# A list scheduler's priorities and durations, and the queue of some DMAs

## Chip, core and metric

The kernel runs on one core of a Trainium2 chip. The metric is the device time in microseconds (us); lower is better. The engines are TensorE (PE), VectorE (DVE), ScalarE (ACT), GpSimd (POOL) and SyncE (SP); ACT and SP also issue DMAs, each on a queue of its own. Each engine runs its own instructions in the order in which the program wrote them, and semaphores join the engines.

## What is computed

The reference takes q, k, v of 2 batches x 8 heads x 768 positions x 64 features, computes hash-bucketed attention, and passes the result through two MLPs.

```python
q_bits = (np.einsum('bhsd,dk->bhsk', q, proj) > 0)   # 6 bits, the same for k
mask = q_bucket[:, :, :, None] == k_bucket[:, :, None, :]
scores = np.where(mask, scale * np.matmul(q, kT), -1e9)
attn = exp(scores - max(scores)); attn = attn / (sum(attn) + 1e-9)
x = np.matmul(attn, v)                               # to 1536 tokens x 512
xn = x / sqrt(mean(x * x) + 1e-6) * rms_g
x = (silu(xn @ w_gate) * (xn @ w_val)) @ w_out       # d_ff 1536
h = maximum(x @ w_in, 0)
out = (h * h) @ w_out2                               # d_ff 2048
```

## The kernel before

**The work.** Attention is cut into 96 slots: 16 heads (`B*H`) by 6 tiles of 128 queries (`QT`). For each head, `plan_prep` plans the loads of k and q (`load_k`, `load_q`), their split into a high and a low part (`split_k1`, `split_q1`, `split_k2`, `split_q2`), a copy of q by DMA (`copy_q`), the product with the hash vectors (`hash_pe`), the threshold that writes the hash bits beside q (`hash_bits`), a DMA that carries k's bits beside k (`hash_dma`), and the load and scaling of v. For each slot, `plan_slot` plans the scores S (`st_S`), their maximum on DVE (`st_min`), the bias (`st_bias`), the exp (`st_exp`), the turning of the probabilities, and the product with v (`st_PV`). A slot of kind "a" splits its probabilities on ACT and POOL (`st_hi`, `st_lo`) and turns them by a DMA transpose on SP's queue (`st_T`); one of kind "x" turns them on TensorE (`st_TP`) and splits them on ACT and DVE (`st_TH`, `st_TL`).

After the eight heads of a batch, `plan_norm` computes the RMS norm (squares, a power on POOL, four small DVE steps, three diagonal scalings in `scales`, and products on TensorE that turn x). Then `products` runs through the two MLPs, with weights that `plan_weights` loads as 64-bit numbers and turns into two 32-bit parts on ACT and DVE. The first batch's MLP overlaps the second batch's attention.

**The order.** `plan_all` adds each operation to a `Plan`: a function, a rank (its priority; the unit is one slot), what it reads and writes, and the time that it is planned to take on each engine that may run it (T, D, A, P, S for TensorE, DVE, ACT, POOL, SP). `Plan.run` is a list scheduler: again and again it takes, among the operations that are ready, the one that could start first on some engine, and of equals the one of lower rank:

```python
best = (t, o.rank), n, eng, c
```

A cost given as a pair, such as `D=(0.47, H_K)`, adds its second number to the time from which that engine may be chosen. `port=True` marks operations that keep DVE and POOL from running at once in the plan. The order found is then written out: each engine gets its instructions in the planned order, and on the chip they start when their semaphores allow, whatever the planned times were. So a planned duration acts through order and choice of engine alone.

Before the change the rank of each operation comes from some 25 constants (`R_LOAD`, `R_S` and so on), the same for all heads or slots. Loads of k and q and the hash-bit DMA of heads 2 and on are issued by ACT (`LQ`, `KQ`; the hash bits from head 1), and are planned at 0.1 us of ACT each:

```python
return {"dma": cost, name: 0.475 if name == "S" else 0.1}
```

Of the kernel before, what the change touches and what calls it, by code (L numbers as in the profile page):

```python
# [23 lines left out]
RQ, RK = 64, 96  # L24
# [35 lines left out]
G = 2  # L60
# [31 lines left out]

W0 = 16
# [11 lines left out]
LQ = 'A'  # L105
KQ = 'A'
WQ = 'S'
VQ = 'S'
QQ = 'S'
# [10 lines left out]
class Plan:  # L120
# [10 lines left out]
    def __init__(self, caps):  # L131
        self.ops, self.tokens, self.bufs, self.chains, self.caps = [], {}, {}, {}, dict(caps)

    def op(self, fn, rank, r=(), w=(), new=(), use=(), dma=0.0, caps=None, chain=None, port=None,
           **costs):
# [4 lines left out]
        )  # L140
        if chain:
            o.after.add(self.chains.get(chain))
            self.chains[chain] = o
# [43 lines left out]

    def run(self):
        free = dict.fromkeys("TDAPS", 0.0)
# [6 lines left out]
        while ready:  # L196
# [22 lines left out]
            c = c[0] if isinstance(c, tuple) else c  # L219
            if o.dma:  # L220
                line = max(t + 1.25, line) + o.dma
                o.end = line
                free[eng] = line - 0.95 if c == "T" else t + c
            else:
                o.end = t + c
                if eng:
                    free[eng] = o.end
                if o.port and eng in port:
                    port[eng] = o.end
# [13 lines left out]
def tile_hash_attention_moe(  # L243
# [81 lines left out]
    def dma(name, cost):  # L325

        return {"dma": cost, name: 0.475 if name == "S" else 0.1}
# [46 lines left out]
    def plan_idle(b, r, rank, cost):  # L374

        def pe(eng):
            nc.tensor.matmul(mo(), idle[:, 0:128], idle, start=True, stop=True)

        add(pe, rank, r=r, new=[("mo", b)], T=cost)
# [5 lines left out]
    def load_k(eng, h):  # L385
        engine[eng].dma_start(out=tile_of(h, "rk", RAW, F32), in_=k[h // H, h % H])
# [269 lines left out]
    def plan_prep(h):  # L656

        s0 = QT * h
        queue = LQ if h > 1 else "S"
        add(lambda e: load_k(e, h), s0 + R_LOAD, new=[("rk", ("rk", h))], **dma(queue, 1.092))  # L660
        add(
            lambda e: load_q(e, h), s0 + R_LOAD + 0.1, new=[("rq", ("rq", h))],
            w=["begun"] * (h == 1), **dma(queue, 0.546),
# [12 lines left out]
            **(dict(D=(0.47, H_K), A=0.733, P=0.8) if h == 0 else dma(QQ, 0.6)),  # L676
        )
        for n, c in enumerate((slice(0, TB), slice(TB, S)) if h == 0 else (slice(0, S),)):
# [5 lines left out]
                P=1.8*f,  # L684
# [4 lines left out]
                P=1.8*f,  # L689
# [16 lines left out]
        else:  # L706
            b = ("hash", h)
            add(
                lambda e: hash_pe(e, h), s0 + R_HASH, T=1.4, use=[("k1", h)],
# [3 lines left out]
                lambda e: hash_bits(e, h), s0 + R_HASH, D=0.87, r=["more"] * (s_ring(h * QT + h) == "Sb"), use=[b, ("q2", h)], w=[("bits", h)],  # L713
# [3 lines left out]
                use=[("k2", h), ("q2", h)], w=[("head", h)], **dma(KQ, 0.1),  # L717
            )
        if h % VG == 0:
            add(  # L720
                lambda e: load_v(e, h), s0 + R_VL, r=["begun"] * (h > 0), new=[("vr", ("vr", h))],
                **dma(VQ if h else "S", 1.092),
            )
            for n in range(VG):
                add(
                    lambda e, n=n: bound_v(e, h, n), s0 + R_VB, use=[("vr", h)],
                    w=[("vb", h, n)], D=0.469,
                )
# [24 lines left out]
    def plan_slot(i):  # L753
# [6 lines left out]
            chain="S", T=0.72, w=[("S", i)],  # L760
        )
        if i < W1:
# [3 lines left out]
            w=[("m", i)], r=["more"] * (i < XEND), D=0.945,  # L766
        )
        add(lambda e: st_bias(e, i), i + R_BIAS, r=[("m", i)], w=[("b", i)], A=0.18, D=(0.08, H_B))
# [3 lines left out]
        if c == "x":  # L772
            for hf in range(2):
# [3 lines left out]
                    use=[("P", i)], new=[("mo", b)], T=0.35,  # L777
# [3 lines left out]
                    new=[("T" + c, ("T", i))] * (1 - hf), w=[("hi", i, hf)], A=0.39,  # L781
# [6 lines left out]
        else:  # L788
# [7 lines left out]
                **dict(P=1.7),  # L796
# [9 lines left out]
            use=[("T", i), ("vl", hx)] + [("O", hx)] * (tx > 0), w=[("PV", hx)], chain="PV",  # L806
            new=[("O", ("O", hx))] * (tx == 0), T=0.54,
# [179 lines left out]
    def plan_weights(m, rank):  # L987
        add(
            lambda e: w_load(e, m), rank, r=["begun"], new=[("wraw", ("wraw", m))],
            **dma(WQ, 1.456),  # L990
# [249 lines left out]
    def plan_all():  # L1240
# [4 lines left out]
        add(lambda e: nc.sync.dma_start(out=cst, in_=small), -40, w=["cst"], **dma("S", 0.056))  # L1245
# [102 lines left out]
```

## Time and profile before

| | |
|---|---|
| median of 3 runs | 823.69 us (823.62 to 825.3) |
| the profiled execution: its time | 821.74 us |
| the profiled execution: its span | 819.5 us |
| granted TensorE clock, mean over the span | 0.985 |
| busy: PE, DVE, ACT, POOL | 778.5, 689.3, 459.3, 220.2 us |

The span goes from the first instruction to the last; the time has some 2 us more around it. Busy times are sums over the whole span, and the kernel has stages with different limits, so they are to be read stage by stage. Issuing a DMA is not counted as busy. "PEld" is the loading of weights into TensorE, which overlaps its products. A granted clock of 1.00 is 2.4 GHz; its other level is 1.2 GHz, and a number between them is a mean over a stretch.

### The profile page before, as it was taken

Reading aid. Unit: us, or ns where it says so; the run is one execution under the profiler, and the core shown is the slowest. Engines: PE = TensorE matmul, PEld = TensorE weight load, DVE = VectorE, ACT = ScalarE, POOL = GpSimd, SP = SyncE. Lnnn points to the kernel's source line nnn. Section 1 sums busy time; section 2 is a strip of 40 time slices with the busy share of each in tenths; the row PEclk is TensorE's granted clock in tenths of the full one; section 3 lists DMA queues with packets and bytes.
Section 4 is the critical chain, followed back from the end, with each engine's and each line's share of the span. In section 5 each row is a group of like instructions: output and inputs, shape, how many; then the busy total and the mean of one; then the engine's idle time right before and its main releaser. Section 6 shows DMA issues by size and latency. Waiting matters only on the chain.

```text
span 819.5 us, 14924 instructions
## 1 busy us (share of the span) xinstructions
PE 778.5 (95%) x5633; PEld 724.0 (88%) x5633; DVE 689.3 (84%) x1369; ACT 459.3 (56%) x931; POOL 220.2 (27%) x187
## 2 busy tenths in 40 slices
PE   7889887999999898999999999999999999999998
PEld 4888776899888897999989999999899899998996
DVE  6997979899888889999998989999487797777764
ACT  5888878768788777443554433466534242342320
POOL 7488956457557544000000000000000000000000
PEclk8999999899999999999999999999999999999999
DMA  7576884689969998232253333422221130211004
GB/s 215 164 133 147 164 181 125 129 173 184 248 146 193 180 198 189 78 103 103 103 180 129 104 128 105 154 104 103 76 79 52 52 104 26 78 52 52 26 1 154
DMA packets 127728, 100.69 MB, mean 123 GB/s; under 512 B 106548, under 2 KB 108596, under 8 KB 127656
## 3 DMA queue, kind: packets, MB, share of 16 engines
q1 hardware_dynamic: 124160, 90.92, 43.4%
q10 hardware_dynamic: 3496, 8.81, 3.7%
q8 instruction: 44, 0.72, 0.4%
q14 instruction: 28, 0.23, 0.1%
HBM read 67.12 MB, written 3.15 MB: 86 GB/s over the span
## 4 chain that ended last, share of the span: by engine, by line
PE 71%; DVE 18%; ACT 3%; DMA 3%; issue 3%; POOL 1%; SPq 0%; ACTq 0%; DVEq 0%; POOLq 0%
PE mo L1012 34%; PE mo L1132 16%; PE mo L1121 9%; PE S L549 5%; PE O L623 4%; DVE Pa L560 2%; DVE Px L560 2%; DMA wraw<-in_w 1%; DVE Tx L314 1%; DVE q L437 1%; PE S L428 1%; PE mo L878 1%; ACT xall L645 1%; DMA Ta<-hla 1%; DVE acc L1146 1%
## 5 line engine op out<-in xcount | busy, mean ns | idle before, releaser
L314 POOL TENSOR_TENSOR hla<-Pa,hla 128x768 f16<-128x768 f32 x66 | 110.0, 1669 | 69.9 <-ACT hla L305 62.9
L1146 DVE TENSOR_TENSOR acc<-acc,mo 128x512 f32<-128x512 f32 (+1 forms) x164 | 101.2, 617 | 27.7 <-PE mo L1132 23.1
L549 PE MATMUL S<-k,q 76*128 76x384 f32 (+1 forms) x384 | 93.2, 368 | 12.9 <-DVE Pa L560 7.3
L1045 ACT ACTIVATE mt<-mo 128x384 f32<-128x384 f32 x64 | 31.4, 490 | 103.8 <-PE mo L1012 101.6
L309 POOL TENSOR_SCALAR yh<-mu 128x384 fp32r<-128x384 f32 x19 | 11.4, 602 | 276.3 <-PE mo L1132 152.4
L549 PEld LDWEIGHTS S<-k,q 76*128 76x128 f32 (+1 forms) x384 | 66.8, 196 | 19.9 <-DVE Pa L560 9.4
L1132 PE MATMUL mo<-woh,yl 128*128 128x512 f32 x192 | 75.3, 392 | 0.0
L1132 PE MATMUL mo<-wol,yh 128*128 128x512 f32 x192 | 75.2, 392 | 0.0
L1132 PE MATMUL mo<-woh,yh 128*128 128x512 f32 x192 | 74.7, 389 | 0.0
L560 DVE TENSOR_SCALAR_CACHE_REDUCE Pa<-S 128x768 f32<-128x768 f32 x66 | 62.7, 950 | 9.2 <-PE S L549 8.6
L956 ACT ACTIVATE wv<-wraw 128x512 f32<-128x512 f32 x82 | 54.1, 669 | 22.5 <-DMA wraw<-in_w 21.7
L1049 DVE TENSOR_TENSOR mu<-mt 128x384 f32<-128x384 f32 x64 | 35.4, 553 | 36.5 <-ACT mt L1045 36.5
L314 DVE TENSOR_TENSOR yl<-mu,yh 128x384 fp32r<-128x384 f32 x112 | 60.8, 551 | 6.0 <-POOL yh L309 4.4
L1121 PE MATMUL mo<-yl,woh 128*128 128x384 f32 x192 | 64.9, 338 | 0.6 <-DVE yl L314 0.6
L1121 PE MATMUL mo<-yh,woh 128*128 128x384 f32 x192 | 65.2, 340 | 0.0
L1121 PE MATMUL mo<-yh,wol 128*128 128x384 f32 x192 | 65.0, 338 | 0.0
L578 ACT ACTIVATE Pa<-Pa,b 128x768 f32<-128x768 f32 x66 | 62.0, 943 | 4.4 <-DVE sum L638 0.9
L305 ACT CAST hla<-Pa 128x768 f16<-128x768 f32 x66 | 55.0, 835 | 4.6 <-DVE sc L509 1.2
L976 DVE SCALAR_TENSOR_TENSOR wv<-wraw,wv 128x512 uint32<-128x512 uint32 x82 | 57.2, 699 | 0.4
L305 ACT CAST wih<-wv 128x512 fp32r<-128x512 f32 x42 | 26.2, 623 | 55.8 <-DVE wv L976 55.5
L972 DVE SCALAR_TENSOR_TENSOR wv<-wraw,wv 128x512 uint32<-128x512 uint32 x82 | 56.4, 690 | 0.7
L1012 PE MATMUL mo<-xTAh,wih 128*128 128x384 f32 x160 | 54.4, 340 | 0.0
(170 smaller groups left out, 2285.7 us busy)
## 6 DMA issues: line engine op xcount, KB each, us to landing
wraw<-in_w SPq DMA_DIRECT2D x104, 512.0 KB
rk<-in_k ACTq DMA_DIRECT2D x14, 384.0 KB
vr<-in_v SPq DMA_DIRECT2D x8, 384.0 KB
out<-acc SPq DMA_DIRECT2D x12, 256.0 KB
q<-q SPq DMA_DIRECT2D x15, 192.0 KB
rq<-in_q ACTq DMA_DIRECT2D x14, 192.0 KB
Ta<-hla SPq DMA_TRANSPOSE x66
rk<-in_k SPq DMA_DIRECT2D x2, 384.0 KB
```

Of the source, the lines that this page charges most:

```text
L305: nc.scalar.copy(out_, in_)
L314: engine[eng].tensor_tensor(out=out_, in0=in0, in1=in1, op=ALU.subtract)
L549: nc.tensor.matmul(sp[:, hf, 0:TB], d[a][0:kr, t * 128:(t + 1) * 128], d[b2][0:kr, hf * TB:(hf + 1) * TB], start=(n == 0), stop=(n == 1),)
L560: nc.vector.tensor_scalar(out=e["P"].rearrange("p (a b) -> p a b", a=2), in0=e["sp"][:, :, 0:TB], scalar1=-1e9 / SCALE, scalar2=None, op0= ...
L578: nc.scalar.activation(e["P"], e["P"], AF.Exp, bias=e["b"], scale=SCALE)
L956: nc.scalar.activation(t, f32(wst[m]["hi"]), AF.Abs)
L972: nc.vector.scalar_tensor_tensor(out=t, in0=hi, scalar=0xC0000000, in1=t, op0=ALU.bitwise_and, op1=ALU.bitwise_or)
L976: nc.vector.scalar_tensor_tensor(out=t, in0=lo, scalar=29, in1=t, op0=ALU.logical_shift_right, op1=ALU.bitwise_or)
L1012: nc.tensor.matmul(ps, a[:, c * 128:(c + 1) * 128], b2[:, c, :], start=(c == 0 and n == 0), stop=(c == 3 and n == 2),)
L1121: nc.tensor.matmul(po, a[:, dc * 128:(dc + 1) * 128], b2, start=(j == 0 and n == 0), stop=(j == len(fs) - 1 and n == 2),)
L1132: nc.tensor.matmul(po, a[:, tt * 128:(tt + 1) * 128], b2, start=(j == 0 and n == 0), stop=(j == len(fs) - 1 and n == 2),)
L1146: nc.vector.tensor_tensor(out=ac, in0=ac, in1=st["p"], op=ALU.add)
```

## The change

The planned durations of some operations are changed, and DMA issues on ACT get planned durations of their own. Loads of k and q and the hash-bit DMA may be issued by SP, or by ACT where its start, with `H_ACT` = 3.0 us added, is earlier. A plan keeps account of narrow and wide products on TensorE and adds `SWITCH` where a wide one follows a narrow one. All engines are planned free from 0.72 us. A table, `SHIFTS`, holds one 16-bit number for each planned operation; divided by 32 it is added to the operation's rank (`Plan.shift`). It has 3,212 numbers, of which 2,159 are not zero; the last of these is number 2,179.

```diff
--- before.py
+++ after.py
@@ -1,4 +1,6 @@
+import base64
 import math
+import zlib
 from collections import deque
 from contextlib import ExitStack
 
@@ -90,6 +92,7 @@
 R_AFT = -10.9
 
 
+SWITCH = 0.085
 W0 = 16
 W1 = 13
 
@@ -102,11 +105,64 @@
 H_K = 2.7
 H_V = 1
 H_VL = 2.0
-LQ = 'A'
-KQ = 'A'
-WQ = 'S'
-VQ = 'S'
-QQ = 'S'
+H_ACT = 3.0
+
+
+SHIFTS = (
+    'c-rk(_jgs*v!A{9Dfiwa5K%y?fK;i%L#6p80x>iNgP?#QEkH#0ieLdkF-WNT6(JCc2nt9OkYYe7Dj<mTA}s+Wgb-o~x1'
...
+)
 
 
 class Op:
@@ -130,14 +186,16 @@
 
     def __init__(self, caps):
         self.ops, self.tokens, self.bufs, self.chains, self.caps = [], {}, {}, {}, dict(caps)
+        self.wide = None
 
     def op(self, fn, rank, r=(), w=(), new=(), use=(), dma=0.0, caps=None, chain=None, port=None,
-           **costs):
+           wide=True, **costs):
 
 
         o = Op(
             fn, rank, costs, dma, new, use, caps or {}, chain, "P" in costs if port is None else port
         )
+        o.wide = wide
         if chain:
             o.after.add(self.chains.get(chain))
             self.chains[chain] = o
@@ -185,8 +243,16 @@
                     t = max(t, u.end + self.delay(u, eng))
         return t
 
+    def shift(self):
+        raw = zlib.decompress(base64.b85decode(SHIFTS)) if SHIFTS else bytes(2 * len(self.ops))
+        assert len(raw) == 2 * len(self.ops)
+        for n, o in enumerate(self.ops):
+            moved = int.from_bytes(raw[2 * n:2 * n + 2], "little", signed=True)
+            o.rank = (round(o.rank * 32) + moved) / 32 + n % 97 * 1e-6
+
     def run(self):
-        free = dict.fromkeys("TDAPS", 0.0)
+        self.shift()
+        free = dict.fromkeys("TDAPS", 0.72)
         line = 0.0
         port = {"D": 0.0, "P": 0.0}
         taken = {ring: [] for ring, _, _ in self.bufs.values()}
@@ -217,6 +283,9 @@
             o = ready.pop(n)[0]
             o.eng, o.start = eng, t
             c = c[0] if isinstance(c, tuple) else c
+            if eng == "T":
+                c += SWITCH * (o.wide and self.wide is False)
+                self.wide = o.wide
             if o.dma:
                 line = max(t + 1.25, line) + o.dma
                 o.end = line
@@ -322,9 +391,9 @@
     def junk():
         return pers.tile([128, 512], F32, tag="wv", name="wv", bufs=WV)
 
-    def dma(name, cost):
-
-        return {"dma": cost, name: 0.475 if name == "S" else 0.1}
+    def dma(cost, act=None, sync=0.475):
+
+        return {"dma": cost, "S": sync, **({"A": (act, H_ACT)} if act else {})}
 
 
     banks = deque([mops] * 3)
@@ -376,7 +445,7 @@
         def pe(eng):
             nc.tensor.matmul(mo(), idle[:, 0:128], idle, start=True, stop=True)
 
-        add(pe, rank, r=r, new=[("mo", b)], T=cost)
+        add(pe, rank, r=r, new=[("mo", b)], T=cost, wide=False)
 
     def tile_of(h, name, n=3, dtype=F32R):
         t = heads[h][name] = ap.tile([128, S], dtype, tag=name, name=name, bufs=n)
@@ -656,11 +725,14 @@
     def plan_prep(h):
 
         s0 = QT * h
-        queue = LQ if h > 1 else "S"
-        add(lambda e: load_k(e, h), s0 + R_LOAD, new=[("rk", ("rk", h))], **dma(queue, 1.092))
-        add(
-            lambda e: load_q(e, h), s0 + R_LOAD + 0.1, new=[("rq", ("rq", h))],
-            w=["begun"] * (h == 1), **dma(queue, 0.546),
+        begun = ["begun"] * (h > 1)
+        add(
+            lambda e: load_k(e, h), s0 + R_LOAD, r=begun, new=[("rk", ("rk", h))],
+            **dma(1.092, 0.42 if h > 1 else None),
+        )
+        add(
+            lambda e: load_q(e, h), s0 + R_LOAD + 0.1, r=begun, new=[("rq", ("rq", h))],
+            w=["begun"] * (h == 1), **dma(0.546, 0.55 if h > 1 else None, 0.55),
         )
         add(
             lambda e: split_k1(e, h), s0 + R_K1, use=[("rk", h)], new=[("k1", ("k1", h))],
@@ -673,7 +745,7 @@
         add(
             lambda e: copy_q(e, h), s0 + R_QC, use=[("rq" if h == 0 else "q1", h)],
             new=[("q2", ("q2", h))], w=[("qc", h)],
-            **(dict(D=(0.47, H_K), A=0.733, P=0.8) if h == 0 else dma(QQ, 0.6)),
+            **(dict(D=(0.47, H_K), A=0.733, P=0.8) if h == 0 else dma(0.6)),
         )
         for n, c in enumerate((slice(0, TB), slice(TB, S)) if h == 0 else (slice(0, S),)):
             f = 0.55 if h == 0 else 1.0
@@ -681,12 +753,12 @@
                 lambda e, c=c: split_k2(e, h, c), s0 + R_K2, use=[("rk", h), ("k1", h)],
                 r=[("k2", h)] if n else [], w=[("k2", h, n)] + [("k2", h)] * (n == 0),
                 new=[("k2", ("k2", h))] * (n == 0), D=(0.87 * f, H_SUB), port=True,
-                P=1.8*f,
+                P=1.9 * f,
             )
             add(
                 lambda e, c=c: split_q2(e, h, c), s0 + R_Q2, use=[("rq", h), ("q1", h)],
                 w=[("ql", h, n)], D=(0.87 * f, H_SUB), port=True,
-                P=1.8*f,
+                P=1.9 * f,
             )
         if h == 0:
             for hf in range(2):
@@ -706,25 +778,25 @@
         else:
             b = ("hash", h)
             add(
-                lambda e: hash_pe(e, h), s0 + R_HASH, T=1.4, use=[("k1", h)],
+                lambda e: hash_pe(e, h), s0 + R_HASH, T=1.39, use=[("k1", h)],
                 r=["wz", ("ql", h, 0), ("k2", h, 0)], new=[(s_ring(h * QT + h), b)],
             )
             add(
-                lambda e: hash_bits(e, h), s0 + R_HASH, D=0.87, r=["more"] * (s_ring(h * QT + h) == "Sb"), use=[b, ("q2", h)], w=[("bits", h)],
+                lambda e: hash_bits(e, h), s0 + R_HASH, D=1.117, r=["more"] * (s_ring(h * QT + h) == "Sb"), use=[b, ("q2", h)], w=[("bits", h)],
             )
             add(
                 lambda e: hash_dma(e, h), s0 + R_HDMA, r=[("bits", h)],
-                use=[("k2", h), ("q2", h)], w=[("head", h)], **dma(KQ, 0.1),
+                use=[("k2", h), ("q2", h)], w=[("head", h)], **dma(0.1, 0.82, 0.8),
             )
         if h % VG == 0:
             add(
                 lambda e: load_v(e, h), s0 + R_VL, r=["begun"] * (h > 0), new=[("vr", ("vr", h))],
-                **dma(VQ if h else "S", 1.092),
+                **dma(1.092),
             )
             for n in range(VG):
                 add(
                     lambda e, n=n: bound_v(e, h, n), s0 + R_VB, use=[("vr", h)],
-                    w=[("vb", h, n)], D=0.469,
+                    w=[("vb", h, n)], D=0.462,
                 )
             b = ("vb", h)
             add(
@@ -757,15 +829,15 @@
         ko = [(x, h) for x in ("k1", "q1", "k2", "q2")]
         add(
             lambda e: st_S(e, i), i + R_S, use=ko, r=[("head", h), ("qc", h)] + [("bits", 0, 1, 0)] * (h == 0 and t >= TT), new=[(s_ring(i), ("S", i))],
-            chain="S", T=0.72, w=[("S", i)],
+            chain="S", T=0.7, w=[("S", i)],
         )
         if i < W1:
             plan_idle(("idle S", i), [("S", i)], i + R_S, 0.22)
         add(
             lambda e: st_min(e, i), i + R_MIN, use=[("S", i)], new=[("P" + c, ("P", i))],
-            w=[("m", i)], r=["more"] * (i < XEND), D=0.945,
-        )
-        add(lambda e: st_bias(e, i), i + R_BIAS, r=[("m", i)], w=[("b", i)], A=0.18, D=(0.08, H_B))
+            w=[("m", i)], r=["more"] * (i < XEND), D=0.9,
+        )
+        add(lambda e: st_bias(e, i), i + R_BIAS, r=[("m", i)], w=[("b", i)], A=0.105, D=(0.08, H_B))
         add(
             lambda e: st_exp(e, i), i + R_EXP, r=[("b", i)], use=[("P", i)], w=[("exp", i)], A=0.827
         )
@@ -774,11 +846,11 @@
                 b = ("PT", i, hf)
                 add(
                     lambda e, hf=hf: st_TP(e, i, hf), i + R_TP, r=[("exp", i), "ident"],
-                    use=[("P", i)], new=[("mo", b)], T=0.35,
+                    use=[("P", i)], new=[("mo", b)], T=0.327, wide=False,
                 )
                 add(
                     lambda e, hf=hf: st_TH(e, i, hf), i + R_TH, r=space, use=[b] + [("T", i)] * hf,
-                    new=[("T" + c, ("T", i))] * (1 - hf), w=[("hi", i, hf)], A=0.39,
+                    new=[("T" + c, ("T", i))] * (1 - hf), w=[("hi", i, hf)], A=0.357,
                 )
                 add(
                     lambda e, hf=hf: st_TL(e, i, hf), i + R_TL, r=[("hi", i, hf)],
@@ -793,7 +865,7 @@
             add(
                 lambda e: st_lo(e, i), i + R_LO, r=[("hi", i)], use=[("P", i), ("hl", i)],
                 w=[("lo", i)], D=(0.87, H_PLO), port=True,
-                **dict(P=1.7),
+                P=1.63,
             )
             add(
                 lambda e: st_T(e, i), i + R_T, r=[("lo", i)] + space,
@@ -803,8 +875,8 @@
         lows = [("lo", i, 0), ("lo", i, 1)] if c == "x" else []
         add(
             lambda e: st_PV(e, i), i + R_PV, r=[("v", hx)] + space + lows,
-            use=[("T", i), ("vl", hx)] + [("O", hx)] * (tx > 0), w=[("PV", hx)], chain="PV",
-            new=[("O", ("O", hx))] * (tx == 0), T=0.54,
+            use=[("T", i), ("vl", hx)] + [("O", hx)] * (tx > 0), w=[("PV", hx)], chain="PV", wide=False,
+            new=[("O", ("O", hx))] * (tx == 0), T=0.548,
         )
         x = i
         m = TT if hx % H == H - 1 else QT
@@ -987,7 +1059,7 @@
     def plan_weights(m, rank):
         add(
             lambda e: w_load(e, m), rank, r=["begun"], new=[("wraw", ("wraw", m))],
-            **dma(WQ, 1.456),
+            **dma(1.456),
         )
         b = ("wv", m)
         far = apart(m)
@@ -1242,7 +1314,7 @@
             nc.vector.memset(warm, 0.0)
             nc.scalar.activation(warm, warm, AF.Exp)
 
-        add(lambda e: nc.sync.dma_start(out=cst, in_=small), -40, w=["cst"], **dma("S", 0.056))
+        add(lambda e: nc.sync.dma_start(out=cst, in_=small), -40, w=["cst"], **dma(0.056))
         add(constants, -40, A=2.3, w=["warm"])
         add(lambda e: nc.vector.memset(idle, 0.0), -40, D=0.1, w=["idle"])
         for n in range(W0):
```

## Rows read from the trace of the kernel before

**Rows 1.** Busy time of each engine by stage: stretch, its length, busy and instructions.

```profile
core 0: us, PE busy (x) PEld busy (x) DVE busy (x) ACT busy (x) POOL busy (x), PEclk, DMA share, GB/s
0.00:13.50 13.50, 8.34 (x26) 3.64 (x27) 7.81 (x27) 5.46 (x8) 8.40 (x15) 0.91 0.62 162
13.50:20.00 6.50, 6.50 (x28) 5.20 (x27) 4.34 (x9) 4.84 (x10) 6.13 (x5) 0.67 1.05 326
20.00:140.00 120.00, 105.05 (x1328) 94.09 (x1326) 105.23 (x229) 103.39 (x240) 82.92 (x69) 0.99 0.70 156
140.00:150.00 10.00, 7.96 (x55) 7.28 (x54) 7.87 (x16) 6.01 (x15) 6.01 (x5) 0.66 0.53 99
150.00:180.00 30.00, 27.82 (x271) 25.97 (x270) 28.12 (x52) 24.17 (x49) 14.91 (x13) 0.94 0.68 142
180.00:340.00 160.00, 149.53 (x1406) 140.60 (x1405) 140.65 (x286) 122.85 (x252) 88.12 (x61) 0.99 0.86 181
340.00:430.00 90.00, 87.57 (x497) 85.42 (x495) 84.56 (x169) 42.56 (x77) 3.25 (x5) 1.00 0.36 123
430.00:815.80 385.80, 385.76 (x2036) 361.77 (x2036) 310.08 (x588) 150.07 (x287) 10.51 (x17) 1.00 0.24 82
815.80:819.50 3.70, 0.00 (x0) 0.00 (x0) 0.69 (x1) 0.00 (x0) 0.00 (x0) 1.00 0.37 142
```

**Rows 2.** Timeline of TensorE at 150 us: start, length, line, operation.

```profile
149.95 0.33 PE L1012 MATMUL mo<-xTAh,wih 128*128 128x384 f32 x1
```

**Rows 3.** ACT's DMA issues by line: shortest, median, longest ns; first and last start.

```profile
L386 ACTq DMA_DIRECT2D rk<-in_k x14: 329/333/359, 10.7 to 211.4; - x14
...
L389 ACTq DMA_DIRECT2D rq<-in_q x14: 473/514/1128, 0.9 to 213.2; - x14
...
L445 ACTq DMA_DIRECT2D k<-q x15: 736/788/1335, 23.8 to 272.7; - x15
```

**Rows 4.** DMA queues from 20 to 140 us: packets, MB, share; and one issue.

```profile
q1 hardware_dynamic: 32263, 12.66, 53.0%
q10 hardware_dynamic: 2332, 5.86, 16.4%
...
k<-q ACTq DMA_DIRECT2D x9, 36.0 KB
```

**Rows 5.** Timeline of ACT at 83 us, with one hash-bit issue.

```profile
83.07 0.94 ACT L578 ACTIVATE Px<-Px,b 128x768 f32<-128x768 f32 x1
84.02 0.75 ACTq L445 DMA_DIRECT2D k<-q  x1
84.88 0.94 ACT L578 ACTIVATE Pa<-Pa,b 128x768 f32<-128x768 f32 x1 [0.86 <-DVE sum L638]
```

**Rows 6.** Instructions grouped by line and form: busy us, mean ns, idle before.

```profile
L314 POOL TENSOR_TENSOR hla<-Pa,hla 128x768 f16<-128x768 f32 x66 | 110.0, 1669 | 69.9 <-ACT hla L305 62.9 <-issue 4.6 <-DMA rk<-in_k 1.8
...
L314 POOL TENSOR_TENSOR k<-rk,k 128x768 fp32r<-128x768 f32 x13 | 24.2, 1858 | 5.7 <-DVE k L307 3.7 <-ACT k L305 1.7
...
L314 POOL TENSOR_TENSOR q<-rq,q 64x768 fp32r<-64x768 f32 x13 | 23.7, 1826 | 1.2 <-ACT q L305 0.3
...
L437 DVE TENSOR_SCALAR q<-S,cst 44x768 fp32r<-44x768 f32 x15 | 16.3, 1086 | 3.3 <-PE S L428 3.0
```

**Rows 7.** Waits of SP's queue: us in total, times, longest.

```profile
SPq L943 <- DVE wv L976: 381.8, 75, 19.6
SPq L590 <- POOL hla L314: 93.6, 39, 6.8
```

**Rows 8.** Timeline of SP's queue at 120 us.

```profile
120.59 2.13 SPq L590 DMA_TRANSPOSE Ta<-hla  x1
```

**Rows 9.** Waits of TensorE from 20 to 140 us.

```profile
PE S L549 <- DVE q L437: 4.4, 7, 1.5
```

**Rows 10.** Timeline of DVE at 140 us.

```profile
140.14 3.49 DVE L869 TENSOR_SCALAR diag<-ident,rr 128x128 f32<-128x128 f32 x3
```

**Rows 11.** Chain of waits at 415 us: start, us, what.

```profile
414.74 3.73 DMA wraw<-in_w
```

52 lines of the change are left out of this document (added).

## Prediction

> **What bounds the kernel now.** I read the stage table first. [rows 1] cuts the span of 819.5 us where the work changes. TensorE idles 819.5 - 778.5 = 41.0 us, and nearly all of it lies early: 5.2 us before 13.5 us, 15.0 between 20 and 140, 4.2 between 140 and 180, 10.5 between 180 and 340, 2.4 between 340 and 430, then 0.04 in 386 us, and 3.7 in the last store. From 430 us on TensorE alone sets the time, and no order of its fixed work can shorten that stretch. A better order can win only before it.
>
> Between 20 and 140 us the attention of the first eight heads runs, and the first product of the MLP cannot start before it is normalised; the first one stands at 149.95 us [rows 2]. In this stage no engine's busy time fills the 120 us: DVE has 105.2, TensorE 105.1, ACT 103.4, POOL 82.9. But issuing a DMA holds an engine without counting as busy. ACT issues three for each head, with medians of 0.333 (k), 0.514 (q) and 0.788 us (hash bits) [rows 3]; nine of each fall into this stage [rows 4], so 9 x 1.635 = 14.7 us. [rows 5] shows one: exp ends, a hash-bit issue of 0.75 us stands alone, ACT is idle for 0.86 us, and the next exp follows. The releaser named there (DVE sum) is the last semaphore seen, not the cause. Busy and issuing together, ACT has 118.1 of 120 us: ACT sets this stage. Between 180 and 340 us no engine is so full: TensorE 149.5 of 160, DVE 140.7, ACT 122.9 [rows 1], with TensorE's idle time spread over waits of about a microsecond.
>
> **The change, part by part.** All arithmetic stays: the same instructions with the same shapes. The edits move instructions between queues and in the order of each queue.
>
> *Planned durations.* The old plan gives ACT 0.1 us for each DMA issue; the rows above say 1.635 us a head, so the old plan misses about 1.3 us of ACT in each of 14 or 15 heads. The new one takes 0.42, 0.55 and 0.82. It raises the hash threshold from 0.87 to 1.117 us (measured 1.086) and the k2/q2 subtractions on POOL from 1.8 to 1.9 (1.858 and 1.826), and lowers POOL's low half from 1.7 to 1.63 (1.669) [rows 6]. These alone cost nothing on the chip; they make the order fit better, and I give them no term of their own.
>
> *Queues.* k, q and the hash bits now take SP unless ACT could start over 3 us earlier (H_ACT). Where SP is busy with transposes some stay on ACT. If all leave, ACT falls to 103.4 us in the first stage and DVE, at 105.2, is next. DVE cannot fill a stage wholly: the densest mixed stage of [rows 1] is 150 to 180 us, with 28.12 of 30, or 94%. At 94% DVE needs 105.2 / 0.94 = 111.9 us: **8 us** gained of a ceiling of 120 - 105.2 = 14.8; the other end is nothing, if the moved issues stay or their transfers come late. I take 8.
>
> What hides the moved issues is SP's spare time, and SP is an in-order queue too. It waits 93.6 us in 39 waits for POOL's low halves before it can transpose, 2.4 us each and 6.8 at the longest [rows 7]; a transpose then holds it for some 2.1 us [rows 8]. Behind such a wait the three DMAs of a head would be late: k and q are loaded well ahead by their ranks, so they have slack; the hash bits have little, since the head's first S waits for them. Today S waits 4.4 us, in 7 waits, with the hash threshold as releaser [rows 9]. I give this no cost in the sum, because the planner treats SP as in order, and its whole price to a rival.
> In 20 to 140 us SP's queue has 53.0% of the DMA engines' time and ACT's 16.4% [rows 4]. The Trainium skill (DMA: Bandwidth & Descriptors, section on queues, rings and completion order) says that each of the two queues has its own rings, that a ring is consumed in order, and that an engine takes turns between rings. By that, a load moved to SP loses its turn and stands behind the transposes; this speaks against the move, and would take from the 8 us what a late k or q costs. The rows show no such load, so I leave the 8.
>
> *The table.* It holds 3,212 numbers, one for each planned operation; 2,159 are not zero, all among the first 2,180: attention, normalisation and the first part of the MLP. Half of these move a priority by more than 25.8 slots (there are 96 slots). A priority decides only between operations that could start at the same moment on an engine, so this is a new choice almost everywhere before about 430 us, and none after. Its gain is bounded by the idle time and lost clock of the stages.
> - 140 to 180 us: idle 4.2 us, and a granted clock of 0.66 over 10 us and 0.94 over 30, worth 3.4 + 1.8 = 5.2 us at full clock: together 9.4. Three diagonal scalings hold DVE for 3.49 us [rows 10], and the chain square, power, scaling, product stays as it is; only other heads' work can fill the gap. I take **4 us**, under half.
> - 180 to 340 us: idle 10.5 us, clock loss 160 x 0.01 = 1.6. With DVE at 94% instead of 88% its 140.7 us would fit in 149.6, also 10.4 less. Both are ceilings; I take **5 us**.
> - 340 to 430 us: 2.4 us idle, as weights land late (3.73 us in the chain [rows 11]). Their loads stay on SP, where they wait 381.8 us in 75 waits for DVE to free a buffer [rows 7], and the later ones have a zero in the table: 0, between 0 and 2.4.
> - 0 to 20 us: the first loads and their order of need are the same: 0, within 2 us either way.
>
> *Narrow and wide products.* SWITCH adds 0.085 us to the plan where TensorE goes from a narrow product to a wide one. It costs the chip nothing; the search can now see that switches cost.
>
> **The sum.** 8 + 4 + 5 = 17 us: a span of 802.5 us. Around the span lie 821.74 - 819.5 = 2.24 us, so the profiled execution would take 804.7; it stood 1.95 us below the median of 823.69, so the median would be 806.7. I forecast 806.
>
> **The rivals.**
> *Slower: the SP queue.* Hash bits behind a transpose that waits for POOL. It speaks for it that SP waits so often, and against it that the plan models the order. If each of 15 heads loses half of a mean wait, 1.2 us, with nothing to cover it, that is 18 us; the first stage's 8 go too, the 9 of the others stay: 823.7 - 9 + 18 = 833. At 17 / 15 = 1.1 us a head, against the whole 17, it decides the sign.
> *No change: the plan doesn't hold on the chip.* A table found in a model fits its errors. The three scalings are still planned at 0.2 us each, against 3.49 in all [rows 10]; such stretches, not in the plan, shift everything behind them, and the in-order queues cannot reorder. Then the old waits are replaced by new ones of the same total: 822 to 824. A part of it, with 2 to 8 us left of the gain, gives 816 to 822.
> *Much faster.* If the search packs all stages to their ceilings: 14.8 + 9.4 + 12.1 + 2.4 = 38.7 us, so 785; with most of it, about 790. For it speaks the number of operations that it moves, against it that DVE and TensorE would both have to be full.
> TensorE's 105.1 us busy between 20 and 140 stand beside 94.1 us of weight loads, and 149.5 beside 140.6 between 180 and 340 [rows 1]. The Trainium skill (Trainium Kernel Development and Optimization, section on performance expectations) calls matmul busy time a bad metric and weight-load busy time a good one. By that the third stage has 160 - 140.6 = 19.4 us to give instead of 10.5, and the ceiling falls by 9 us to 776. DVE stops the stage first by the rows, so I count 0.02 of this case's chance to it.
>
> **Chances.** Forecast, a gain of 8 to 26 us (798 to 816): 0.60. Much faster: 0.12. A small gain (816 to 822): 0.10. No change: 0.06. Slower: 0.12. A measurement of this kernel tells about 0.2%, or 1.6 us, from no change. So faster 0.82, same 0.06, slower 0.12. The range of 790 to 822 leaves out the slower case, half of no change and a little of the ceiling: 2 in 10. The likeliest case's own range is 798 to 816.
>
> **What would show it.** Right: under half of the 27 ACT issues left in the first stage; the first MLP product at about 140 us instead of 150; TensorE's idle time down from 41 to some 25 to 28 us, with the stretch after 430 as long as before for the same products; fewer stretches below full clock before 240 us. Wrong: SP's waits grow and S waits longer for the hash bits (the queue rival); ACT is relieved, but DVE's idle time grows as much (the model rival); or the first product comes earlier but the weights or DVE hold TensorE up after 340 us, so that the gain is given back later.

## The result, and the profile after

The changed kernel takes 804.81 us (median of 4 runs, 800.63 to 807.46) against 824.50 us for the kernel before beside it (4 runs, 823.62 to 826.37). The ratio is 0.9754, with a 95% interval of 0.9707 to 0.9800: a gain of 19.7 us, where 17 were forecast. The profiled execution took 800.63 us, with a span of 798.8. It is the fastest of the four, so what its stages show lies on the good side; a second profiled execution of the same kernel (the changed kernel again, below), with a span of 805.8, is named beside it.

The stages of the changed kernel, in the columns of [rows 1]:

```profile
0.00:13.50 13.50, 11.07 (x39) 5.64 (x39) 9.94 (x32) 5.43 (x7) 8.80 (x15) 1.00 0.58 162
13.50:20.00 6.50, 3.48 (x20) 2.79 (x21) 3.79 (x9) 4.05 (x8) 4.15 (x4) 1.00 0.96 305
20.00:140.00 120.00, 110.92 (x1368) 100.00 (x1369) 109.34 (x242) 112.71 (x264) 94.37 (x78) 0.96 0.77 166
140.00:150.00 10.00, 10.00 (x103) 9.52 (x102) 9.38 (x19) 7.02 (x11) 5.47 (x5) 1.00 0.81 116
150.00:180.00 30.00, 27.88 (x257) 26.64 (x254) 29.50 (x56) 21.39 (x43) 17.00 (x13) 1.00 0.91 216
180.00:340.00 160.00, 152.05 (x1422) 144.98 (x1422) 142.02 (x286) 119.84 (x243) 86.53 (x65) 1.00 0.81 169
340.00:430.00 90.00, 90.00 (x522) 90.00 (x521) 85.90 (x173) 46.39 (x86) 3.32 (x5) 1.00 0.38 130
430.00:795.10 365.10, 365.05 (x1918) 341.06 (x1917) 291.76 (x555) 137.66 (x264) 12.27 (x20) 1.00 0.24 81
795.10:798.80 3.70, 0.00 (x0) 0.00 (x0) 0.68 (x1) 0.00 (x0) 0.00 (x0) 0.96 0.37 142
sum 798.80, PE 770.46 PEld 720.62 DVE 682.31 ACT 454.50 POOL 231.90; mean PE 85.61 PEld 80.07 DVE 75.81 ACT 50.50 POOL 25.77
```

Read the last long stretch first. From 430 us on TensorE is full, as before: 365.10 / 1918 = 0.190 us for each of its instructions, and 385.80 / 2036 = 0.189 before [rows 1]. Nothing was gained there; 118 of these instructions had simply been done already. So the whole gain was made before 430 us.

How much in which stage? TensorE loses time in two ways: by standing idle, and by running below its full clock, which is the length times one less the granted clock (at most that, since idle time inside the stretch is counted in both). Fixed stretches of time cut the work of the two kernels at different places (the normalisation of the first batch moved from beyond 140 us to before it), so the first four stretches are taken together:

| TensorE's loss, us | before: idle + clock | after: idle + clock | gained |
|---|---|---|---|
| 0 to 150 | 22.2 + 7.9 | 14.5 + 4.8 | 10.8 |
| 150 to 340 | 12.7 + 3.4 | 10.1 + 0.0 | 6.0 |
| 340 to 430 | 2.4 + 0.0 | 0.0 + 0.0 | 2.4 |

That is 19.2 of the span's 20.7 us; the clock is shown to two digits only. The second execution gives 6.6, 2.2 and 2.4 us by the same count, 11.2 of the 13.7 by which its span is shorter. Each part loses less in both; how much each gives differs by several us. Over the whole span idle time went from 41.0 to 28.3 us (32.3 in the second execution), and the mean clock from 0.985 to 0.993 (0.989).

The DMA issues that ACT still has between 20 and 140 us, from its timeline:

```profile
29.22 0.33 ACTq L455 DMA_DIRECT2D rk<-in_k  x1
73.34 0.49 ACTq L458 DMA_DIRECT2D rq<-in_q  x1
110.01 0.33 ACTq L455 DMA_DIRECT2D rk<-in_k  x1
```

Three are left of 27 [rows 4]: 1.2 us in place of 14.7. ACT is nevertheless still the fullest engine of the stage. Its busy time rose from 103.4 to 112.7 us, because 264 instructions now fit instead of 240. With its issues that makes 113.9 of 120 us, or 95%; TensorE has 110.9, or 92%, and DVE 109.3, or 91%. Cut where the norm's first squares begin (below), the stage shows what the issues did: before, ACT has 98.6 us of its own work and 14.7 of issues in the 115.2 us from 20 us on; after, 100.9 and 1.2 in 105.7. ACT fills 98% of the first stretch and 97% of the second. It had some 11 us less to do, and the stretch is 9.5 shorter.

The waits of SP's queue in the changed kernel, to be held against [rows 7]:

```profile
SPq L1015 <- DVE wv L1048: 387.7, 74, 19.6
SPq L659 <- POOL hla L383: 53.7, 30, 5.2
```

And TensorE's wait for the hash bits from 20 to 140 us, against [rows 9]:

```profile
PE S L618 <- DVE q L506: 0.4, 1, 0.4
```

SP's waits for POOL's low halves fell from 93.6 to 53.7 us although it took over the issues (in the first experiment below, which keeps the old order, they are 55.0, so the fall goes with the move), and S waits for hash bits for 0.4 us instead of 4.4.

Two marks of progress, by line: the squares of the RMS norm on ACT, which begin as soon as the attention of the first half of the first batch's positions is done, and the first kind of MLP product (shortest, median, longest ns; first and last start in us):

```profile
L912 ACT ACTIVATE wv<-xall x12: 614/630/657, 125.7 to 325.1; 128x512 f32<-128x512 f32 x12
...
L1084 PE MATMUL mo<-xTAh,wih x160: 333/334/427, 144.8 to 775.9; 128*128 128x384 f32 x160
```

The squares begin at 125.7 us; before it was 135.2. The first product starts at 144.8 instead of 149.95 [rows 2]. (In the second execution they stand at 128.2 and 147.9.) Of 9.5 us won by the squares, 4.4 don't show at the first product: 19.1 us lie between the two now, 14.7 before. But the first product does not mark the same progress in both kernels. The norm is done in two halves of three tiles of positions each, and the first MLP product on the second half (xTB) has moved much further:

```profile
L1012 PE MATMUL mo<-xTBh,wih x160: 332/334/423, 170.0 to 798.7; 128*128 128x384 f32 x160
...
L1084 PE MATMUL mo<-xTBh,wih x160: 332/334/423, 147.5 to 778.0; 128*128 128x384 f32 x160
```

It starts at 147.5 instead of 170.0. The new order puts the whole second half of the norm ahead of the first product, the 24 products that turn its x too; before, these ran between 160 and 170 us:

```profile
141.37 2.25 PE L950 MATMUL mo<-diag,xall 128*128 128x128 f32 x18
...
144.17 0.83 PE L950 MATMUL mo<-diag,xall 128*128 128x128 f32 x6
```

So the longer way to the first product holds work that came later before. POOL lengthens it as well, as this stretch of DVE and POOL shows:

```profile
136.64 0.15 DVE L929 TENSOR_TENSOR rt<-rr 128x3 f32<-128x3 f32 x1
136.83 1.50 DVE L931 TENSOR_TENSOR rt<-rt,ss 128x3 f32<-128x3 f32 x1
138.36 1.58 DVE L933 TENSOR_SCALAR rt<-rt 128x3 f32<-128x3 f32 x1
139.97 0.81 DVE L937 TENSOR_TENSOR rr<-rr,rt 128x3 f32<-128x3 f32 x1
140.89 0.68 DVE L941 TENSOR_SCALAR diag<-ident,rr 128x128 f32<-128x128 f32 x3
141.49 0.61 DVE L387 SCALAR_TENSOR_TENSOR xTAl<-mo,cst,xTAh 128x384 fp32r<-128x384 f32 x1
...
136.66 3.25 POOL L383 TENSOR_TENSOR hla<-Pa,hla 128x768 f16<-128x768 f32 x2
139.86 0.90 POOL L383 TENSOR_TENSOR vl<-vr,ones 128x384 f16<-128x384 f32 x1
```

Four steps on three columns take 0.14 to 0.16 us each where nothing holds them (the kernel before, from 138.60 to 140.11 us), as the first one does here. The second ends at 138.33, half-way through POOL's pair of subtractions. The third ends at 139.94, as the pair ends at 139.91; the fourth at 140.78, as POOL's next one ends at 140.76. These steps belong to the second half of the norm, but DVE's queue is in order, and the low parts of the turned x (xTAl), which the first product needs, stand behind them.

### The profile page after: what moved, and what is told of

It reads as the page before. It is cut to its first block, busy times and chain, and to the rows that moved or that the text cites. A ratio compares the mean times of both kernels' runs of the same rounds, so it can differ in the third digit from the quotient of the medians.

```text
span 798.8 us, 14938 instructions
## 1 busy us (share of the span) xinstructions
PE 770.5 (96%) x5633; PEld 720.6 (90%) x5633; DVE 682.3 (85%) x1365; ACT 454.5 (57%) x922; POOL 231.9 (29%) x200
## 4 chain that ended last, share of the span: by engine, by line
PE 59%; DVE 0%; ACT 0%; issue 0%
PE mo L1084 33%; PE mo L1204 16%; PE mo L1193 9%; PE mo L950 1%; DVE acc L1218 0%; ACT xall L714 0%
## 5 line engine op out<-in xcount | busy, mean ns | idle before, releaser
L1218 DVE TENSOR_TENSOR acc<-acc,mo 128x512 f32<-128x512 f32 (+1 forms) x164 | 100.9, 618 | 28.4 <-PE mo L1204 23.1
L618 PE MATMUL S<-k,q 76*128 76x384 f32 (+1 forms) x384 | 87.1, 354 | 7.3 <-DVE Pa L629 6.2
L618 PEld LDWEIGHTS S<-k,q 76*128 76x128 f32 (+1 forms) x384 | 65.0, 190 | 10.8 <-DVE Pa L629 8.3
L378 POOL TENSOR_SCALAR yh<-mu 128x384 fp32r<-128x384 f32 x25 | 14.1, 569 | 199.9 <-PE mo L1204 88.4
L383 DVE TENSOR_TENSOR yl<-mu,yh 128x384 fp32r<-128x384 f32 x112 | 65.4, 590 | 6.1 <-POOL yh L378 5.2
L378 POOL TENSOR_SCALAR wih<-wv 128x512 fp32r<-128x512 f32 x11 | 7.2, 658 | 174.1 <-ACT mt L1117 109.7
L1044 DVE SCALAR_TENSOR_TENSOR wv<-wraw,wv 128x512 uint32<-128x512 uint32 x82 | 56.0, 687 | 0.4
L1048 DVE SCALAR_TENSOR_TENSOR wv<-wraw,wv 128x512 uint32<-128x512 uint32 x82 | 55.9, 684 | 0.2
```

The costliest lines, as they stand in the source:

```text
L383: engine[eng].tensor_tensor(out=out_, in0=in0, in1=in1, op=ALU.subtract)
L618: nc.tensor.matmul(sp[:, hf, 0:TB], d[a][0:kr, t * 128:(t + 1) * 128], d[b2][0:kr, hf * TB:(hf + 1) * TB], start=(n == 0), stop=(n == 1),)
L1044: nc.vector.scalar_tensor_tensor(out=t, in0=hi, scalar=0xC0000000, in1=t, op0=ALU.bitwise_and, op1=ALU.bitwise_or)
L1048: nc.vector.scalar_tensor_tensor(out=t, in0=lo, scalar=29, in1=t, op0=ALU.logical_shift_right, op1=ALU.bitwise_or)
L1218: nc.vector.tensor_tensor(out=ac, in0=ac, in1=st["p"], op=ALU.add)
```

## The experiments

All gains below are against the kernel before in the same group of runs: 824.04 us for the first three kernels, 823.00 for the next three, 822.95 for the last four.

**The issues alone, in the order of before.** Every DMA that ACT issues is issued by SP instead, at the same place of the order.

```diff
-            o.fn(o.eng)
+            o.fn("S" if o.dma and o.eng == "A" else o.eng)
```

> The order of the kernel before on every compute engine, but the 43 DMA issues of ACT (k, q, hash bits) are issued by SP at their place in the planned sequence. Theory (ACT's issue time sets the first stage): about 8 us less, 814 to 819 us, with the squares of the first batch starting some 5 to 9 us earlier than 135.2 us. Rival of the SP queue: hash bits come late behind waiting transposes, 825 us or more, S waits longer for the hash bits. Rival that the order alone counts: 822 to 825 us.

Measured: 820.54 us, ratio 0.9962 (0.9930 to 0.9993), a gain of 3.5 us. Its squares by line:

```profile
L840 ACT ACTIVATE wv<-xall x12: 612/620/637, 129.9 to 325.4; 128x512 f32<-128x512 f32 x12
```

They begin 5.3 us earlier than before, with no new plan. TensorE's waits from 20 to 140 us, of which the slower rival spoke:

```profile
PE S L549 <- DVE q L437: 3.4, 5, 1.5
...
PE S L549 <- DMA k<-q: 1.0, 1, 1.0
```

One wait of 1.0 us for a hash-bit transfer, even where nothing was planned for it. Moving the issues pays by itself, clear of no change, but not for the 8 us that were expected.

**The change without the table.**

```diff
-SHIFTS = (
...
-)
+SHIFTS = ""
```

> The changed kernel with all numbers of the table zero: new durations, new choice of queue, old ranks. Theory: keeps the 8 us of the first stage and loses the 9 of the other two, about 813 to 817 us. Rival that the table does it all: 821 us or more. Rival that queues and durations do it all: 804 to 808 us.

Measured: 815.78 us, ratio 0.9893 (0.9851 to 0.9935), a gain of 8.3 us. Durations and queues give these, with the smaller edits that stay in (`SWITCH`, the start at 0.72 us, the `begun` condition on later loads); the table gives the rest. Its squares start at 124.8 us, no later than with the table, and its first product on the second half at 159.1.

**The changed order, with the issues on ACT.** Every DMA that the change lets choose is issued by ACT.

```diff
-            o.fn(o.eng)
+            o.fn("A" if o.dma and "A" in o.costs else o.eng)
```

> The order of the changed kernel on every compute engine, but all k and q loads of heads 2 and on and all hash-bit DMAs are issued by ACT at their place in the sequence. Theory: ACT has 118 us of work again in the first stage, so 8 us or more are lost, 812 to 820 us. Rival that the table alone counts: 804 to 808 us.

Measured: 809.44 us, ratio 0.9824 (0.9768 to 0.9881): 4.6 us above the changed kernel's first series and 3.4 above its longer one (below), both of other groups, and the intervals overlap. So the loss of 8 us or more that was expected did not come. The squares stand where ACT's load puts them:

```profile
L912 ACT ACTIVATE wv<-xall x12: 616/628/656, 131.7 to 331.8; 128x512 f32<-128x512 f32 x12
```

That is 6.0 us later than in the changed kernel, or 3.5 later than in its second execution, against 5.3 us earlier in the first experiment. Both directions say that the issues delay the first batch's attention by 3.5 to 6 us.

**The durations alone.** No table, and the movable DMAs are planned and issued on ACT, with their new durations; the smaller edits named above stay in.

```diff
-        return {"dma": cost, "S": sync, **({"A": (act, H_ACT)} if act else {})}
+        return {"dma": cost, **({"A": act} if act else {"S": sync})}
```

> New durations (0.42, 0.55 and 0.82 us for ACT's issues among them) and SWITCH, table of zeros, k, q and hash-bit DMAs on ACT as before. With the table zero and the choice of queue the time was 815.8 us. Theory: ACT's issues leave the first stage only with the queue, so this gives 818 to 822 us, some 4 us more than with the choice. Rival that honest durations do most of the 8 us by themselves: 814 to 817 us. Rival that durations don't matter: 822 to 826 us.

Measured: 820.75 us, ratio 0.9964 (0.9924 to 1.0004), a gain of 2.3 us that is not clear of nothing. Its squares start at 134.8 us, 0.4 earlier than before: by themselves the durations do not shorten the first stage. The free choice of queue is worth 8.3 - 2.3 = 6.0 us within a plan that knows the durations, a difference of two groups whose intervals overlap a little.

**The table for part of the time.** The shifted ranks are used up to a planned time, and the old ones from there on, once with `CUT = 130` and once with 340.

```diff
+                    rank = o.rank if t < CUT else o.base
...
-                        best = (t, o.rank), n, eng, c
+                        best = (t, rank), n, eng, c
```

Up to 130:

> The changed kernel, but the planner uses the table's ranks only for operations that it places before 130 us of its own clock, and the old ranks after. Bounds from the runs so far: 815.8 us without the table, 804.8 with it. If the table's gain is made in the first stage: 805 to 808 us. If it is made by the overlap of attention and MLP after it, as the prediction's 4 + 5 us say: 812 to 817 us.

Up to 340:

> As the one before, with the table's ranks until 340 us of the planner's clock and the old ranks after. If the table's gain lies before the pure MLP stretch: 803 to 808 us, as with the whole table. If its last part, which orders the first part of the MLP, matters: 809 us or more.

Measured: 814.59 us (0.9806 to 0.9936) up to 130, a gain of 8.4; 805.55 us (0.9709 to 0.9812) up to 340, a gain of 17.5. Used up to 130 us the table adds next to nothing to the 8.3 us without it. Its use from 130 to 340 us adds 9.0 us to that, and the runs of the two kernels lie apart (812.9 to 816.52 and 805.03 to 806.71). Whether the table for 130 to 340 alone would give as much was not tried, nor was any single move of it, so by what moves it wins its 9 us stays open.

**The table on the plan of before.** With the old durations and queues the same table leads to no order at all: at some point every operation that is ready waits for a buffer that none of the ready ones frees. So it has no time, but it shows that these numbers cannot be carried to that plan.

**The changed kernel again**, in the group of the three that follow.

> The changed kernel itself again, as the measure for the other three of this call: 804.8 us, between 800 and 808, since its single runs so far lie that far apart.

Measured: 806.04 us (6 runs, 803.64 to 809.04), ratio 0.9786 (0.9754 to 0.9818), a gain of 16.9 us.

**Without three of POOL's subtractions.** For slots 49 to 51 POOL writes zeros in place of the low half of the probabilities; the rest is unchanged.

```diff
         hl = tiles[i]["hl"]
+        if i in (49, 50, 51):
+            nc.gpsimd.memset(hl[:, 1, :], 0.0)
+            return
         sub(eng, hl[:, 1, :], tiles[i]["P"], hl[:, 0, :])
```

> The changed kernel, with the low half of slots 49, 50 and 51 (the ones that POOL subtracts while the first norm runs) filled with zeros by POOL instead of being computed. Theory (POOL's subtraction of 128x768 holds DVE's small steps of the norm): the steps that take 1.50 and 1.58 us take some 0.15, the first norm's products come 2 to 4 us earlier after the squares, 800 to 803 us. Rival (something else stretches them): the steps stay long, 804 to 806 us.

Measured: 803.16 us (0.9729 to 0.9784), 2.9 us below the unedited kernel of the same group, with intervals that overlap. DVE's steps and POOL in the unedited kernel:

```profile
139.81 1.50 DVE L931 TENSOR_TENSOR rt<-rt,ss 128x3 f32<-128x3 f32 x1
141.34 1.58 DVE L933 TENSOR_SCALAR rt<-rt 128x3 f32<-128x3 f32 x1
...
139.64 3.25 POOL L383 TENSOR_TENSOR hla<-Pa,hla 128x768 f16<-128x768 f32 x2
```

And with the zeros:

```profile
138.62 0.16 DVE L934 TENSOR_TENSOR rt<-rt,ss 128x3 f32<-128x3 f32 x1
138.81 1.06 DVE L936 TENSOR_SCALAR rt<-rt 128x3 f32<-128x3 f32 x1
...
138.44 1.42 POOL L656 MEMSET hla<- 128x768 f16 x2
```

The stretched steps repeat to the digit in another execution, and shrink with POOL's work: that POOL holds DVE there is shown. From squares to first product it is 16.5 us instead of 19.6 in the unedited run, against 14.7 in the kernel before. So POOL's subtractions make some 3 us of that stretch; the rest of the difference is put down to the order.

**The norm planned with POOL.** The four steps and the scalings get `port=True`, which keeps them from lying beside POOL in the plan, and the table is searched anew for that plan.

```diff
-            add(lambda e, n=n: newton(e, hf, n), R_X, r=[("rr", hf)], w=[("rr", hf)], D=0.08)
+            add(lambda e, n=n: newton(e, hf, n), R_X, r=[("rr", hf)], w=[("rr", hf)], D=0.09, port=True)
...
-                D=0.2,
+                D=0.21, port=True,
```

> The planner is told that the three-column steps and the diagonal scalings of the norm can't run beside POOL's work (port), and the table is searched anew for that plan. If the unplanned stretch in the norm is what the changed kernel loses: 797 to 802 us. If a new table is worth no more than the old one on the chip: 803 to 807 us.

Measured: 807.04 us (0.9764 to 0.9839), no better than the changed kernel. On the chip a step still took up to 1.45 us and a scaling up to 1.69, so the plan did not keep them clear of what lengthens them. The table is also another one, and the two cannot be told apart here.

**The table searched further**, with nothing else changed.

> The same planner as in the changed kernel and its table searched further, nothing else. If each step that the search finds is kept on the chip: 800 to 803 us. If further search only fits the plan: 804 us or more, and above the kernel whose plan knows the norm.

Measured: 800.25 us (6 runs, 798.46 to 808.22), ratio 0.9732 (0.9693 to 0.9771): 5.8 us below the changed kernel in the same group, with intervals that overlap. It has the lowest median of all versions here.

## Why the prediction held, point by point

**Where time can be won: right.** Nothing was won after 430 us, and TensorE's loss before it fell in every part. Idle time ended at 28.3 us in one execution and 32.3 in the other, where some 25 to 28 were named. Of the stretches of 5 us before 240 us, 10 lay below full clock before, and 3 and 5 after.

**The first stage, 8 us: the size was right, the reason only in part.** Durations and queues together measured 8.3 us, and the first half of the argument holds: ACT set the stage, and the issues were what it could lose. The step "ACT's issues leave, and DVE is next at 94%" failed in its second half. ACT remained the fullest engine, at 95%, and DVE stands at 91%. Nor is 94% a limit for DVE: in the changed kernel it has 29.50 of the 30 us from 150 to 180, or 98%. The 8 came from that limit, so its nearness to 8.3 is partly luck. The removal by itself is worth 3.5 us (first experiment); the other side gave 3.4 to 4.6, not clear of noise. The new durations, to which the prediction gave no term, gave 2.3 by themselves, not clear of noise either. The rest is put down, by difference only, to letting the planner choose the queue while it makes the order.

**The table, 4 + 5 = 9 us: right in size and place.** It measured 16.9 - 8.3 = 8.6 us by the longer series of the changed kernel and 19.7 - 8.3 = 11.4 by the first one, and the cut at 130 and 340 puts it where the two terms lay. How it divides at 180 us was not measured. The two terms were taken as about half of their ceilings, not worked out from what the table moves, so their sum was a good guess rather than an account. The whole, 17 us against 19.7 and 16.9, is nearer than its parts.

**340 to 430 us, 0: mis-sized.** The 2.4 us of idle time there are gone, in both executions. TensorE's named waits there before were for DVE's low parts of weights (1.8 us) and of y (0.6). Without the table the stretch still has 4.0 us of idle time. That more products done ahead took the waits away is only argued.

**0 to 20 us, 0 within 2: not settled.** TensorE's idle time and lost clock there fell from 8.5 to 5.5 us in one execution and to 7.5 in the other.

**The first product at about 140 us: wrong**, 144.8 (147.9 in the second execution). The prediction let the chain from squares to product stay as it is; it left out that the new order puts the second half of the norm in front, and POOL. It read the 3.49 us of the three scalings [rows 10] as a fixed length of the path. It is POOL's: in the kernel before POOL has, over the same time,

```profile
140.11 3.24 POOL L314 TENSOR_TENSOR hla<-Pa,hla 128x768 f16<-128x768 f32 x2 [1.75 <-ACT hla L305]
```

and it ends at 143.35, as the scalings end at 143.63. In the changed order the same three scalings, those of the first half, take 1.65 us, and the first step ahead of them 1.00, up to the end of a subtraction of POOL at 131.61:

```profile
130.63 1.00 DVE L929 TENSOR_TENSOR rt<-rr 128x3 f32<-128x3 f32 x1
...
132.53 1.65 DVE L941 TENSOR_SCALAR diag<-ident,rr 128x128 f32<-128x128 f32 x3
...
129.96 1.65 POOL L383 TENSOR_TENSOR hla<-Pa,hla 128x768 f16<-128x768 f32 x1
```

In the second half the scalings take 0.68 us, and POOL holds the steps ahead of them instead. Over both halves the eight steps and six scalings take DVE 7.3 us before and 8.1 after. The hold was moved, not removed. TensorE meanwhile falls idle and then below full clock, as before. In stretches of 5 us of the changed kernel:

```profile
125.00:130.00 5.00, 3.35 (x47) 2.76 (x46) 4.63 (x15) 4.97 (x16) 3.08 (x4) 1.00 0.66 102
130.00:135.00 5.00, 3.38 (x29) 2.72 (x30) 4.96 (x16) 3.52 (x9) 3.83 (x5) 0.79 0.67 170
135.00:140.00 5.00, 5.00 (x25) 5.00 (x24) 3.97 (x9) 4.01 (x8) 4.73 (x5) 0.53 0.10 20
140.00:145.00 5.00, 5.00 (x53) 4.83 (x52) 4.83 (x10) 3.37 (x6) 2.07 (x2) 1.00 0.75 139
```

TensorE is busy for 3.35 and 3.38 of 5 us in the first two of these. The granted clock is 0.53, near the lower of its two levels, from 135 to 140, just as the first half's products that turn x run.

**The slower rival** fell: SP's waits for POOL's low halves shrank, and even the unplanned move of the first experiment met one wait of TensorE, of 1.0 us, for hash bits. All engines' waits for loads of k and q, over the whole span, are 11.4 us before and 11.7 after. The rule on rings that the prediction weighed against the move (the Trainium skill, DMA: Bandwidth & Descriptors) took nothing that these rows show.

**No change, because the plan doesn't hold:** its mechanism is there (steps planned at 0.08 us take up to 1.58), its price is not. Taking POOL's part in it away at the first norm gave 2.9 us, not clear of noise, beside a gain of some 17 to 20.

**Much faster** was not reached. The longer search suggests that part of the distance was open, though its interval overlaps with the changed kernel's. The measure by weight loads is not decided: from 180 to 340 us they rose from 140.60 to 144.98 us, and the products from 149.53 to 152.05.

**The resolution was too fine.** The prediction took 0.2%, or 1.6 us, from three runs. The kernel before spans 11.6 us over the later groups (see the end), so the gain as a whole is clear, and most single terms are not.

## What to carry to other kernels

Before asking which engine is full, add the DMA issues to its busy time; then price the move of these issues by emitting the same order on another queue, since that separates them from everything that a new plan does. Expect a searched table of priorities to fit the plan in which it was found: here it gave no order at all on the one other plan that was tried. Before taking one instruction's start as the mark of progress, look at what the new order has put in front of it. And where a small instruction takes many times its shortest duration, look for the end of another engine's instruction at its own end before taking the length as the instruction's.

## What the runs showed of the hardware

**POOL can hold DVE's smallest steps for whole instructions.** Steps of 0.15 us took 1.50 and 1.58 and ended with POOL's instruction. Beside a POOL instruction that only writes, the step with two inputs (L934 there) took 0.16 us and the one with a scalar operand (L936) 1.06, again until POOL's end (139.87 and 139.86 us). The Trainium skill (SBUF — State Buffer, section "Who interferes with whom") has this as an exclusive lock: a DVE instruction with two SBUF inputs is held up by a GpSimd instruction that reads SBUF and not by one that only writes it, while a DVE tensor_scalar, where it runs in a mode that uses two ports, contends with GpSimd either way. The rows agree on each point; in which mode the step ran no row shows.

**Which DMA is issued matters more than its bytes.** The 36 KB of hash bits hold the issuing engine for 0.788 us, a k load for 0.333 [rows 3]. The Trainium skill (DMA: Bandwidth & Descriptors, section "Issuing engines are not separate DMA queues") says that issuing from several engines saves only the sequencer's time, "which is usually small relative to the DMA itself". Here that time was 14.7 of 120 us on the engine that set the stage, and its removal alone gave 3.5 us of the kernel (a ratio of 0.9930 to 0.9993).

**One program's executions differ by about 1%.** The changed kernel's 10 runs span 800.63 to 809.04 us; the kernel before, which spanned 823.62 to 826.37 in 4 runs, spans 820.36 to 831.93 in the 37 of the three later groups. So single differences of 3 to 6 us above are only as good as their intervals. In the two profiled executions of the changed kernel ACT's first instruction on k, which waits for its load, starts at 4.12 and at 5.07 us, the squares at 125.7 and 128.2, and the spans are 798.8 and 805.8. That a late first load sets off the rest is only argued; no run held all else equal.
